# Exponentials of the windowed attention on one engine or two, two more borrowed load buffers, and an even cut of the widest score row

## The chip, the cores and the metric

The kernel runs on 1 core of one Trainium2 chip. The metric is device time in microseconds (us), the median over runs of the whole kernel. The engines are PE (matrix multiplications and transposes), DVE (vector), ACT (scalar functions), POOL and SP (which only issues DMA here).

## The reference, cut to what matters

Three layers follow one another, over 4 batches of 576 positions with model width 512.

- **Windowed attention**, 8 heads of width 64. Heads 0 to 3 see the 32 positions up to their own; heads 4 to 7 see every fourth of the 128 positions up to their own. `attn = exp(scores - max) / (sum + 1e-9)`, then `attn @ v`.
- **A mixture of 4 causal attention experts** (head width 64, all 576 positions): `q = x @ wq[e]`, `scores = q @ k.T / 8`, causal mask, softmax, `@ v @ wo[e]`. A gate takes the best 2 of 4 experts for each position and weights them by a softmax.
- **A normalized MLP** with residual: `x + relu(norm(x) @ w_ch1) @ w_ch2`, hidden width 2048.

Everything is computed in float32. A large product is made as three products of a high and a low part (hence names such as `xh` and `xl`, `wkh` and `wkl`).

## The kernel before, in words

**One list orders everything.** The program is written as many small generators, called chains, one for each piece of work: `turned_qk`, `scores`, `window` for the windowed layer, `project`, `attend`, `out_proj` for the experts, `decode`, `norm_tile`, `mlp_group` for the MLP. Each step of a chain names an engine, a planned duration and the times of what it depends on. `run_chains` keeps a planned clock for each engine (`free`) and always emits the step that can start first; the rank of the chain breaks ties. The planned durations therefore decide in which order each engine gets its instructions, and on the chip each engine works through its own order and waits where a dependence is late. A step made with `either(...)` may go to one of two engines; the list compares their start times and takes the first named where they are equal. PSUM is handed out as 8 banks by `acq("bank")` and `give_bank`.

**Windowed layer.** Work goes by head pair `hp` (0 to 3) of batch `b`. `load_qk` loads q and k of a pair (288 KB each) from SP into two tiles tagged `nat`; there are two such tiles in all, so the next pair waits until the transposes of `turned_qk` (line 442) have read this one. For batch 0, pairs 1 and 2 use pieces 0 to 7 of `x2a` instead, which holds the mixture's output later. `load_v` loads v into one of two `vt` places and waits for a place that the multiplications by v (line 565) of an earlier pair have left. `all_loads` is one chain: its loads stand in SP's queue in a fixed order, pair by pair, q and k before v. `landing` plans when a load has arrived: 600 ns, then 4.76 ns for each KB behind the loads before it, then 1200 ns. `turned_qk` transposes q and k and copies them (`ptr` to `qT`, `kT`) by ACT or DVE; `scores` (lines 490 to 504) forms the masked scores of a pair in two banks; `window` handles one of the two halves `u`, so there are 4 x 4 x 2 = 32 such blocks. A block has 6 groups of 80 columns (dilated pairs) or 5 or 4 groups of 96 columns. In each: DVE takes the maximum of each group (line 525) and subtracts it (527), ACT takes the exponential of the whole block (530), DVE sums and inverts (532, 534), DVE or POOL multiplies (536), PE transposes (548), ACT or DVE copies (251), PE multiplies by v (565), ACT and DVE split the result into `xh` and `xl` (579, 581).

**Experts.** `project` makes queries and keys (line 706), `value_tile` values and gate logits (605), and `attend` handles one block of 128 queries for two experts. The last block (i = 4) has 576 columns and does not fit one bank of 512, so its scores (lines 778, 779, mask 781) are cut in two: columns 0 to 64 and 64 to 576, with a maximum (801) and an exponential (806) for each. There are 2 x 2 x 4 = 16 such rows of scores. `out_proj` (929) writes pieces of `x2a`.

**MLP.** Lines 1157 and 1179; it begins while the last batch's experts still run.

Of the kernel before, what the change touches and what calls it, by code (L numbers as in the profile page):

```python
# [23 lines left out]
def windowed_attention_moe_mlp(  # L24
# [37 lines left out]
    QB = 8  # L62
    SCALE = 0.125
    DQ, DW = 48, 80
    NBD = S // DQ

    def qrange(i):
# [97 lines left out]
    def op(engine, ns, deps=(), tile=None):  # L165
        return "op", ((engine, ns),), deps, tile
# [4 lines left out]
    def acq(tag, n=1):  # L171
        return "acq", tag, n
# [4 lines left out]
    def give(tag, at, n=1):  # L177
        places[tag] += [at] * n

    def give_bank(b, at):  # L180
        places["bank"].append((at, lent_banks.pop(id(b))[0]))
# [7 lines left out]
    def act(n, psum=True):  # L189
        return (55.0 if psum else 100.0) + 0.835 * n  # L190

    def dve(n):
        return 65.0 + 1.045 * n

    def turn(n):
        return 0.834 * n + 2.5
# [7 lines left out]
    def run_chains():  # L204
        while chains:
            again = True
            while again:
                again = False
                for c in sorted(chains, key=lambda c: c[0]):
                    kind = c[2][0]  # L210
                    if kind == "acq" and len(places[c[2][1]]) >= c[2][2]:
                        tag, n = c[2][1:]
                        places[tag].sort()
                        at = places[tag][n - 1]
                        if tag == "bank":
                            taken.extend(x for _, x in places[tag][:n])
                            at = at[0]
                        del places[tag][:n]
                        resume(c, at)
                        again = True  # L220
                        break
                    if kind == "key" and c[2][1] in facts:
                        resume(c, facts[c[2][1]])
                        again = True
                        break
            best = None
            for c in chains:
                if c[2][0] != "op":
                    continue
                _, engines, deps, tile = c[2]  # L230
                for name, ns in engines:
                    engine = name.rstrip("*")
                    at = max([free[engine]] + [d + lag[engine] for d in deps])
                    if name != engine:
                        at = max(at, shared["POOL" if engine == "DVE" else "DVE"])
                    change = MODE if engine == "PE" and tile != mode[0] else 0.0
                    score = (at + change + (ns if len(engines) > 1 else 0.0) * 0.0, c[0])
                    if best is None or score < best[0]:
                        best = score, c, name, ns, at + change, tile
            assert best is not None, [(c[0], c[2]) for c in chains]  # L240
            _, c, name, ns, at, tile = best
            engine = name.rstrip("*")
            if name != engine:
                shared[engine] = at + ns + 80.0
            free[engine] = at + ns
            if engine == "PE":
                mode[0] = tile
            resume(c, (at + ns + tail[engine], engine) if len(c[2][1]) > 1 else at + ns + tail[engine])
# [72 lines left out]

    SLOT = (3, 2, 4, 1, 5, 0, 6, 7, 8)

    def landing(t, kb):

        land[0] = max(t + 600.0, land[0]) + 4.76 * kb
        return land[0] + 1200.0

    def issue(e, dst, src):
# [8 lines left out]
    def load_qk(b, hp, engines="SS"):  # L338
        h0 = 2 * hp
        cw = 8 if h0 >= H // 2 else 6  # L340
        pw = S // cw
        lent = b == 0 and hp in (1, 2)
        t = (yield acq("nat", 2)) if not lent else 0.0
        nats, times = [], []
        for x, src in enumerate((q, k)):
            if lent:
                nat = x2a[:, 4 * hp - 4 + 2 * x:4 * hp - 2 + 2 * x].rearrange("p a n -> p (a n)")
            else:
                nat = win.tile([P, 2 * DM], F32, tag="nat", name="nat", bufs=2)
            nat = nat[:pw, :cw * 2 * D].rearrange("p (c h d) -> p c h d", c=cw, h=2)  # L350
            e = "ACT" if engines[x] == "A" else "SP"
            ti = yield op(e, 780.0, [t])
            issue(e, nat, src[b, h0:h0 + 2].rearrange("h (p c) d -> p c h d", c=cw))
            nats.append(nat)
            times.append(landing(ti, 288.0))
        LD[b, hp] = nats, times
        put("ld", b, hp, at=0.0)
# [65 lines left out]
    def turned_qk(b, hp):  # L423

        yield key("ld", b, hp)
        nats, times = LD[b, hp]
        tq = yield acq("qT")
        qT = win.tile([P, S], F32, tag="qT", name=f"qT{b}_{hp}", bufs=2)
        kT = win.tile([P, W + S], F32, tag="kT", name=f"kT{b}_{hp}", bufs=2)
        yield op("POOL", 130.0, [tq])  # L430
        nc.gpsimd.memset(kT[:, 0:W], 0.0)
        dil = 2 * hp >= H // 2
        cw = 8 if dil else 6
        pw, ch = S // cw, cw // 2
        ends = []
        for x in range(4):
            nat, hf = nats[x // 2], x % 2
            ta = yield acq("bank")
            pt = bank("ptr")
            t = yield op("PE", ch * turn(pw), [ta, times[x // 2]])  # L440
            for c in range(ch):
                nc.tensor.transpose(pt[:, pw * c:pw * (c + 1)],  # L442
                                    nat[:, hf * ch + c].rearrange("p h d -> p (h d)"), ident[:pw, :pw])
            if hf and not (b == 0 and hp in (1, 2)):
                give("nat", t)
            dst = kT[:, W:] if x > 1 else qT
            if dil:
                dst = dst.rearrange("p (c j x) -> p x c j", c=4, x=2)[:, hf]
                sp = pt[:, :HS].rearrange("p (c j) -> p c j", c=4)
            else:  # L450
                dst = dst.rearrange("p (j c) -> p j c", c=cw)[:, :, hf * ch:(hf + 1) * ch]
                sp = pt[:, :HS].rearrange("p (c j) -> p j c", c=ch)
            if x > 1:
                t, e = yield either(("ACT", 345.0), ("DVE", 366.0), deps=[t, tq])
                copy_by(e, dst, sp)
            else:
                t, e = yield either(("ACT", 345.0), ("DVE", 366.0), deps=[t, tq])
                if e == "ACT":
                    nc.scalar.mul(dst, sp, SCALE)
                else:  # L460
                    nc.vector.tensor_scalar(dst, sp, SCALE, None, op0=ALU.mult)
            give_bank(pt, t)
            ends.append(t)
        TQ[b, hp] = qT, kT
        put("qT", b, hp, at=max(ends))
# [44 lines left out]
    def window(b, hp, u):  # L510
# [11 lines left out]
        sc = sx[:, :nb, off:96]  # L522
        mx, sm, rs = [win.tile([P, NBD // NU], F32, tag=x, name=x, bufs=5)[:, :nb] for x in ("mx", "sm", "rs")]
        t = yield op("DVE", dve(kw * nb), [t])
        nc.vector.tensor_reduce(mx, psv, axis=AX.X, op=ALU.max)
        t = yield op("DVE", dve(kw * nb), [t, ts])
        nc.vector.tensor_tensor(sc, psv, mx[:, :, None].to_broadcast([P, nb, kw]), op=ALU.subtract)
        give_bank(ps, t)
        t = yield op("ACT", act(kw * nb, False), [t])
        nc.scalar.activation(sc, sc, AF.Exp)  # L530
        t = yield op("DVE", dve((kw + 1) * nb), [t])
        nc.vector.tensor_reduce(sm, sx[:, :nb, off:], axis=AX.X, op=ALU.add)
        t = yield op("DVE", 85.0, [t])
# [24 lines left out]
        vt, tv, home = LV[b, hp]  # L558
        ta = yield acq("bank")
        po = bank("po")  # L560
        t = yield op("PE", nb * (91.0 if dil else 114.0), ends + [ta, tv], "columns")
        for tt, t_ in enumerate(blk):
            for h in range(2):
                z = side(u, HALVES[h]).start // 64
# [187 lines left out]
    def attend(b, pr_, i):  # L752
# [16 lines left out]
        Pp = att.tile([P, 2, S], F32, tag="P", name="Pp", bufs=DB + 1)  # L769
        Ps, tsum = [], []  # L770
        for ee in range(2):
            cuts = [(0, n)] if n <= 512 else [(0, 64), (64, n)]
            tb = yield acq("bank", len(cuts))
            pss, tss = [bank("s2") for _ in cuts], []
            for (a, z), ps in zip(cuts, pss):
                end = z == n
                t = yield op("PE", 2 * max(0.4415 * (z - a) + 5.0, 90.0) + (55.0 if end else 0.0), [tb, tq])
                nc.tensor.matmul(ps[:m, :z - a], SQ[ee][:, q0:q0 + m], KH[ee][:, a:z], start=True, stop=False)  # L778
                nc.tensor.matmul(ps[:m, :z - a], SQ[ee][:, q0:q0 + m], KL[ee][:, a:z], start=False, stop=not end)  # L779
                if end:  # L780
                    nc.tensor.matmul(ps[:m, q0 - a:z - a], ident_bf, mdiag[:, :n - q0], start=False, stop=True)  # L781
                tss.append(t)
# [123 lines left out]
    def out_proj(b, i):  # L906
# [10 lines left out]
        if ti >= NTA:  # L917

            yield key("fr", b, (ti - NTA) // 2)
        elif HOME[ti] >= LENT:  # L920
            for hp in range(NHP):
                t = max(t, (yield key("x", B - 1, hp)))
# [345 lines left out]
```

## Time and profile before

| what | value |
|---|---|
| median of 3 runs | 723.19 us (722.45 to 726.18) |
| the profiled execution's own time | 725.05 us |
| its span, first to last instruction | 723.3 us |
| mean granted clock of TensorE | 0.995 |
| PE busy in the span | 700.0 us (97%) |
| DVE, ACT, POOL busy | 524.5, 287.0, 165.1 us |

Time outside the span is 725.05 - 723.3 = 1.75 us. Busy time of PE is the time in which some matmul was under way, from its start to its modelled end; matmuls overlap, so the rate is read from one start to the next, not from the duration. In rows of a timeline an idle time before an instruction stands in brackets with what ended it. "SPq" is SP issuing a DMA.

### The profile page before, as it was taken

The numbers are of one execution on the slowest core, as the hardware profiler recorded it, in microseconds if no ns is written. First come the engines' busy times: TensorE is split into PE (matmuls) and PEld (weight loads), VectorE is DVE, ScalarE is ACT, GpSimd is POOL, SyncE is SP. The second block draws the span as 40 slices with busy tenths as digits, with TensorE's granted clock in tenths as the row PEclk, the third lists the DMA queues.
The fourth block names the chain that finished last, engine by engine and source line by source line (L and its number), as shares of the span: only waits on it lengthen the run. The fifth ranks groups of instructions, "written<-read, shape, count | busy, mean of one in ns | idle before, by whom it ended". The sixth has DMA issues, their size and how long they took to land.

```text
span 723.3 us, 13830 instructions
## 1 busy us (share of the span) xinstructions
PE 700.0 (97%) x5396; PEld 588.5 (81%) x5396; DVE 524.5 (73%) x1240; ACT 287.0 (40%) x754; POOL 165.1 (23%) x190
## 2 busy tenths in 40 slices
PE   6799999999999999999999999999999999999997
PEld 4788787988898888877878888888888888888886
DVE  4759879968989999994588874774774865844343
ACT  3566757656656667851242231220221211311100
POOL 3641113110011325220035351230330420410000
PEclk9999999999999999999999999999999999999999
DMA  9953541033312112000002121020110110100123
GB/s 166 200 134 83 115 102 46 18 67 74 82 42 69 38 47 68 30 30 1 1 29 88 59 87 30 30 86 2 59 58 1 61 56 12 47 1 1 58 88 116
DMA packets 78385, 43.10 MB, mean 60 GB/s; under 512 B 60145, under 2 KB 73713, under 8 KB 78321
## 3 DMA queue, kind: packets, MB, share of 16 engines
q1 hardware_dynamic: 78320, 42.23, 23.2%
q8 instruction: 42, 0.69, 0.4%
q14 instruction: 23, 0.18, 0.1%
HBM read 35.14 MB, written 4.72 MB: 55 GB/s over the span
## 4 chain that ended last, share of the span: by engine, by line
PE 84%; DVE 5%; DMA 4%; ACT 3%; SPq 2%; issue 1%; POOL 0%; ACTq 0%; DVEq 0%; POOLq 0%
PE phid L1157 28%; PE pout L1179 28%; PE pp L706 5%; PE pv L605 3%; PE pwo L929 3%; PE ppt L854 2%; DMA nat<-in_q_dram 2%; PE po L565 2%; PE ppt L548 2%; PE py L875 2%; SPq L330 2%; PE s L778 2%; PE s L779 2%; PE ptr L442 2%; PE py L873 1%; PE s L504 1%
## 5 line engine op out<-in xcount | busy, mean ns | idle before, releaser
L1179 PE MATMUL pout<-wp,ht 128*128 128x512 f32 x864 | 220.1, 395 | 0.0
L1157 PE MATMUL phid<-xn,wp 128*128 128x512 f32 (+1 forms) x960 | 218.9, 371 | 0.0
L1157 PEld LDWEIGHTS phid<-xn,wp 128*128 128x128 f32 x960 | 168.8, 188 | 34.4
L1179 PEld LDWEIGHTS pout<-wp,ht 128*128 128x128 f32 x864 | 160.0, 188 | 35.1 <-ACT ht L1162 0.2
L1162 ACT ACTIVATE ht<-phid 128x512 fp32r<-128x512 f32 (+1 forms) x80 | 44.4, 554 | 225.1 <-PE phid L1157 225.1
L1188 DVE SCALAR_TENSOR_TENSOR x2a<-pout,rstd,x2a 128x512 f32<-128x512 f32 x124 | 92.5, 748 | 53.9 <-PE pout L1179 53.1
L1164 DVE SCALAR_TENSOR_TENSOR ht<-phid,ht 128x512 fp32r<-128x512 f32 (+1 forms) x80 | 50.8, 635 | 58.6 <-ACT ht L1162 57.9
L1031 POOL TENSOR_TENSOR d_pw<-d_pw,d_t 128x512 f32<-128x512 f32 x32 | 41.6, 1299 | 184.9 <-DVE d_pw L1028 151.7
L1043 POOL TENSOR_TENSOR wp<-d_pw,wp 128x512 fp32r<-128x512 f32 x32 | 44.3, 1384 | 45.7 <-ACT wp L1041 45.7
L536 POOL TENSOR_TENSOR sc<-sc,rs 128x480 f32<-128x480 f32 (+1 forms) x24 | 22.9, 963 | 88.2 <-DVE rs L534 62.8
L251 ACT COPY pT<-ppt 80x288 f32<-80x288 f32 (+6 forms) x77 | 32.1, 426 | 19.5 <-PE ppt L854 9.9
L1015 ACT ACTIVATE d_sq<-ws 128x512 f32<-128x512 f32 x32 | 21.6, 676 | 44.0 <-DVE d_pw L1034 25.3
L794 ACT ACTIVATE Pp<-s,nm 128x448 f32<-128x448 f32 (+3 forms) x64 | 30.3, 476 | 12.5 <-DVE nm L792 11.5
L1041 ACT CAST wp<-d_pw 128x512 fp32r<-128x512 f32 x32 | 19.9, 621 | 35.6 <-DVE d_pw L1034 32.9
L778 PE MATMUL s<-KH,SQ 128*128 128x64 f32 (+4 forms) x96 | 32.6, 347 | 0.2
L1034 DVE SCALAR_TENSOR_TENSOR d_pw<-d_sq,d_pw 128x512 f32<-128x512 f32 x32 | 22.0, 689 | 14.7 <-POOL d_pw L1031 14.7
L442 PE MATMUL ptr<-ident,nat 72*128 72x72 f32 (+1 forms) x196 | 24.4, 246 | 7.2 <-DMA nat<-in_q_dram 6.4
L548 PE MATMUL ppt<-ident,sc 112*80 112x112 f32 (+1 forms) x168 | 27.2, 282 | 3.9 <-POOL sc L536 2.4
L779 PE MATMUL s<-klz,SQ 128*128 128x64 f32 (+4 forms) x96 | 30.2, 315 | 0.0
L1188 DVE SCALAR_TENSOR_TENSOR x2b<-pout,rstd,x2b 128x512 f32<-128x512 f32 x32 | 24.0, 749 | 8.4 <-PE pout L1179 8.2
L854 PE MATMUL ppt<-ident,Pp 128*128 128x128 f32 x160 | 28.5, 283 | 0.4 <-DVE yl L892 0.2
L792 DVE TENSOR_REDUCE nm<-s 128x1 f32<-128x448 f32 (+3 forms) x64 | 26.3, 415 | 3.1 <-PE s L781 2.3
(166 smaller groups left out, 1294.9 us busy)
## 6 DMA issues: line engine op xcount, KB each, us to landing
ws<-in_moe_w_ch_dram SPq DMA_DIRECT2D x32, 512.0 KB, 3.5
nat<-in_q_dram SPq DMA_DIRECT2D x14, 288.0 KB, 4.0
nat<-in_k_dram SPq DMA_DIRECT2D x14, 288.0 KB, 6.6
out_dram<-x2a SPq DMA_DIRECT2D x12, 256.0 KB, 2.0
KH<-KH SPq DMA_DIRECT2D x32, 72.0 KB, 1.9
vt<-in_v_dram SPq DMA_DIRECT2D x10, 192.0 KB, 3.9
x2a<-in_v_dram SPq DMA_DIRECT2D x8, 160.0 KB
vt<-in_v_dram SPq DMA_DIRECT2D x8, 160.0 KB
```

Source lines behind the costliest of these rows:

```text
L442: nc.tensor.transpose(pt[:, pw * c:pw * (c + 1)], nat[:, hf * ch + c].rearrange("p h d -> p (h d)"), ident[:pw, :pw])
L548: nc.tensor.transpose(pt[:kw, P * (tt - a):P * (tt - a) + pw], sc[:pw, tt], ident[:pw, :pw])
L778: nc.tensor.matmul(ps[:m, :z - a], SQ[ee][:, q0:q0 + m], KH[ee][:, a:z], start=True, stop=False)
L779: nc.tensor.matmul(ps[:m, :z - a], SQ[ee][:, q0:q0 + m], KL[ee][:, a:z], start=False, stop=not end)
L854: nc.tensor.transpose(pt[:, P * (j - 1):P * j], Ps[ee][:, k0:k0 + P], ident)
L1031: nc.gpsimd.tensor_tensor(pf, pf, t1.bitcast(F32), op=ALU.add)
L1043: nc.gpsimd.tensor_tensor(lo, pf, hi.bitcast(F32), op=ALU.subtract)
L1157: nc.tensor.matmul(ph[:, :n_tok], ws[:, c * P:(c + 1) * P], xs[c], start=n == 0, stop=n == 3 * KC - 1)
L1162: nc.scalar.activation(hh[:, :n_tok], ph[:, :n_tok], AF.Relu)
L1164: nc.vector.scalar_tensor_tensor(hl[:, :n_tok], ph[:, :n_tok], 0.0, hh[:, :n_tok].bitcast(F32), op0=ALU.max, op1=ALU.subtract)
L1179: nc.tensor.matmul(po, a_[:, sl], w_, start=n == 0, stop=n == 3 * len(fs) - 1)
L1188: nc.vector.scalar_tensor_tensor(x2(i), po, rstd[:, i:i + 1], x2(i), op0=ALU.mult, op1=ALU.add)
```

## The change

- `window`: the maximum is stored negated. The subtraction on DVE becomes an addition, or the list gives the block to ACT alone, which then takes one exponential for each group, straight out of PSUM, with the negated maximum as bias. The list picks the engine that can start first; `LEAN` is 0, so DVE is taken where both can start at the same time. In the first way the bank is handed back after DVE's addition, in the second after the last exponential.
- `load_qk`: batch 1's pairs 1 and 2 also use pieces 0 to 7 of `x2a`, and wait for the transposes of batch 0's same pair. `out_proj` into these pieces waits until batch 1's pair has been transposed.
- `attend`: the last block's scores are cut into columns 0 to 288 and 288 to 576.
- Planned durations: 5.4 instead of 4.76 ns per KB of a load, and the issuing queue's planned clock is held to 3200 ns before the planned end of its transfers; 25 ns more for the transposes of q and k; 110 instead of 91 ns for each dilated group of the multiplication by v; 100 instead of 55 ns for the score rows' mask.

```diff
     DQ, DW = 48, 80
+    LEAN = 0.0
...
-                for name, ns in engines:
+                for name, ns, *lean in engines:
...
-                    score = (at + change + (ns if len(engines) > 1 else 0.0) * 0.0, c[0])
+                    score = (at + change + sum(lean), c[0])
...
-    def landing(t, kb):
-
-        land[0] = max(t + 600.0, land[0]) + 4.76 * kb
+    def landing(t, kb, e="SP"):
+
+        land[0] = max(t + 600.0, land[0]) + 5.4 * kb
+        free[e] = max(free[e], land[0] - 3200.0)
         return land[0] + 1200.0
...
-        lent = b == 0 and hp in (1, 2)
-        t = (yield acq("nat", 2)) if not lent else 0.0
+        lent = b < 2 and hp in (1, 2)
+        if not lent:
+            t = yield acq("nat", 2)
+        else:
+            t = (yield key("nq", 0, hp)) if b else 0.0
...
-            t = yield op("PE", ch * turn(pw), [ta, times[x // 2]])
+            t = yield op("PE", ch * turn(pw) + 25.0, [ta, times[x // 2]])
...
-            if hf and not (b == 0 and hp in (1, 2)):
+            if hf and not (b < 2 and hp in (1, 2)):
                 give("nat", t)
+            if x == 3:
+                put("nq", b, hp, at=t)
...
-        nc.vector.tensor_reduce(mx, psv, axis=AX.X, op=ALU.max)
-        t = yield op("DVE", dve(kw * nb), [t, ts])
-        nc.vector.tensor_tensor(sc, psv, mx[:, :, None].to_broadcast([P, nb, kw]), op=ALU.subtract)
-        give_bank(ps, t)
-        t = yield op("ACT", act(kw * nb, False), [t])
-        nc.scalar.activation(sc, sc, AF.Exp)
+        nc.vector.tensor_reduce(mx, psv, axis=AX.X, op=ALU.max, negate=True)
+        t, e = yield either(("DVE", dve(kw * nb), 0.0), ("ACT", nb * 222.0, LEAN), deps=[t, ts])
+        if e == "DVE":
+            nc.vector.tensor_tensor(sc, psv, mx[:, :, None].to_broadcast([P, nb, kw]), op=ALU.add)
+            give_bank(ps, t)
+            t = yield op("ACT", act(kw * nb, False), [t])
+            nc.scalar.activation(sc, sc, AF.Exp)
+        else:
+            for tt in range(nb):
+                nc.scalar.activation(sc[:, tt], psv[:, tt], AF.Exp, bias=mx[:, tt:tt + 1])
+            give_bank(ps, t)
...
-        t = yield op("PE", nb * (91.0 if dil else 114.0), ends + [ta, tv], "columns")
+        t = yield op("PE", nb * (110.0 if dil else 114.0), ends + [ta, tv], "columns")
...
-            cuts = [(0, n)] if n <= 512 else [(0, 64), (64, n)]
+            cuts = [(0, n)] if n <= 512 else [(0, HS), (HS, n)]
...
-                t = yield op("PE", 2 * max(0.4415 * (z - a) + 5.0, 90.0) + (55.0 if end else 0.0), [tb, tq])
+                t = yield op("PE", 2 * max(0.4415 * (z - a) + 5.0, 90.0) + (100.0 if end else 0.0), [tb, tq])
...
+        elif ti < 8:
+            t = max(t, (yield key("nq", 1, 1 + ti // 4)))
```

## Rows read from the trace of the kernel before

**Rows 1.** Busy time in stretches: columns PE, PEld, DVE, ACT, POOL, clock, DMA, GB/s.
```profile
82.00:86.00 4.00, 2.52 (x47) 2.08 (x42) 3.36 (x11) 2.20 (x8) 0.99 (x1) 0.77 1.07 217
40.00:250.00 210.00, 203.12 (x2571) 180.30 (x2568) 181.57 (x575) 134.62 (x405) 36.04 (x60) 0.99 0.32 74
370.00:723.30 353.30, 349.40 (x1604) 287.40 (x1602) 220.00 (x333) 68.68 (x122) 83.34 (x65) 1.00 0.15 50
```
**Rows 2.** The page's first part: busy time of PE over the span.
```profile
PE 700.0 (97%) x5396; PEld 588.5 (81%) x5396; DVE 524.5 (73%) x1240; ACT 287.0 (40%) x754; POOL 165.1 (23%) x190
```
**Rows 3.** Waits of PE over the whole span: total us, times, longest.
```profile
PE ptr L442 <- DMA nat<-in_q_dram: 6.4, 3, 5.0
PE ppt L548 <- POOL sc L536: 2.4, 5, 0.8
PE s L504 <- ACT kT L251: 1.5, 1, 1.5
```
**Rows 4.** Timeline of PE, last block's scores in batch 3: start, duration.
```profile
238.84 0.19 PE L778 MATMUL s<-KH,SQ 128*128 128x64 f32 x1
...
238.98 0.47 PE L778 MATMUL s<-KH,SQ 128*128 128x512 f32 x1
239.29 0.39 PE L779 MATMUL s<-klz,SQ 128*128 128x512 f32 x1
239.52 0.23 PE L781 MATMUL s<-mdiag,ident_bf 128*128 128x128 bf16 x1
```
**Rows 5.** Chain of waits, a run of projections with 288 columns: start, length.
```profile
141.21 1.58 PE pp L706 x12
```
**Rows 6.** Groups of instructions by shape on DVE and ACT: busy us, mean ns.
```profile
L527 DVE TENSOR_TENSOR sc<-s,mx 128x480 f32<-128x480 f32 x24 | 15.3, 646 | 0.1
L530 ACT ACTIVATE sc<-sc 128x480 f32<-128x480 f32 x24 | 14.2, 606 | 5.0 <-DVE sc L527 4.8
L794 ACT ACTIVATE Pp<-s,nm 128x192 f32<-128x192 f32 x16 | 6.7, 420 | 4.3 <-DVE nm L792 3.8 <-DVE rs L818 0.4
L794 ACT ACTIVATE Pp<-s,nm 128x64 f32<-128x64 f32 x16 | 5.0, 315 | 1.4 <-DVE nm L792 1.0
```
**Rows 7.** Timelines of DVE and ACT, two such blocks back to back.
```profile
29.35 1.21 DVE L527 TENSOR_TENSOR sc<-s,mx 128x480 f32<-128x480 f32 x2
31.31 1.10 ACT L530 ACTIVATE sc<-sc 128x480 f32<-128x480 f32 x2
```
**Rows 8.** Timeline of ACT and PE around PE's wait for kT.
```profile
81.20 1.10 ACT L530 ACTIVATE sc<-sc 128x480 f32<-128x480 f32 x2
...
82.80 0.78 ACT L251 COPY kT<-ptr 128x288 f32<-128x288 f32 x2
...
83.73 1.13 PE L504 MATMUL s<-kT,qT 64*64 64x96 f32 x29 [1.48 <-ACT kT L251]
```
**Rows 9.** Timeline of SP: loads of batch 1 in the order of the queue.
```profile
31.17 3.72 SPq L330 DMA_DIRECT2D x2a<-in_v_dram  x3
39.55 0.59 SPq L330 DMA_DIRECT2D nat<-in_q_dram  x1
...
47.75 0.84 SPq L330 DMA_DIRECT2D nat<-in_q_dram  x1
...
60.21 1.28 SPq L330 DMA_DIRECT2D x2a<-in_v_dram  x3
61.54 0.86 SPq L330 DMA_DIRECT2D nat<-in_q_dram  x1
```
**Rows 10.** Timeline of PE: batch 1's first scores, then transposes of its pairs 1 and 3.
```profile
44.55 0.23 PE L495 MATMUL s<-mfirst,ident_bf 64*64 64x96 bf16 x2 [0.78 <-DVE xl L581]
...
45.24 0.35 PE L496 MATMUL s<-mgen,ident_bf 64*64 64x384 bf16 x2 [0.30 <-DVE xl L581]
...
46.22 0.30 PE L442 MATMUL ptr<-ident,nat 96*128 96x96 f32 x1
...
67.34 0.44 PE L442 MATMUL ptr<-ident,nat 72*128 72x72 f32 x4 [1.07 <-DMA nat<-in_q_dram]
```

## The prediction

> **What bounds the kernel now.** First the busy time of the engines over the span: PE has a matmul under way for 700.0 of 723.3 us [rows 2], so at most 23.3 us are open gaps. Next the stretches [rows 1]. From 370 us to the end the MLP runs alone, with PE busy for 349.4 of 353.3 us; no edit touches an instruction there. The 32 windowed blocks lie before about 250 us. From 40 to 250 us PE is busy for 203.1 of 210 us, DVE for 181.6 (86%) and ACT for 134.6 (64%). So DVE is the fuller of the two helpers, yet PE sets the pace: work taken off DVE earns only where PE waited for it. An edit can pay in three ways: fewer columns or less dead time on PE itself, a wait of PE that goes, or a stretch at the lower clock that goes.
>
> Then the waits of PE [rows 3]. The largest, 6.4 us for q, holds 5.0 us for the very first load, which nothing here changes; 1.4 us are left. 2.4 us are waits for POOL's multiply, which stands behind DVE's sums. 1.5 us is one wait for a copy of k on ACT, and the timeline shows why [rows 8]: two whole-block exponentials hold ACT from 81.20 us, the copies start at 82.80, PE starts at 83.73. In 82 to 86 us the granted clock is 0.77 [rows 1]. The levels are 1.2 and 2.4 GHz, that is 0.5 and 1.0, so this mean hides a spell at 1.2 GHz, after a gap of PE; it costs up to 4.0 x 0.23 = 0.9 us.
>
> **The even cut of the widest score row.** It happens 16 times. Now four matmuls (two of 64, two of 512 columns) take from 238.84 to the mask at 239.52, that is 0.68 us [rows 4]. The new four have 288 columns each, 1152 in all as before. Twelve of 288 columns take 1.58 us in a dense run [rows 5], so four take 0.53 and save 0.15 us. But the second matmul of the wide pair starts 0.31 us after the first, and the next after it 0.23 us later: there are some 0.08 us of dead time where the shape changes, and part of this may stay. I take 0.10 x 16 = 1.6 us; bounds 0 and 0.15 x 16 = 2.4 us. DVE and ACT see the same columns in the same number of instructions, so I cost that at nothing.
>
> **Exponentials on ACT alone.** Per block that changes side, DVE loses an addition of 0.646 us [rows 6]; two of them take 1.21 us back to back [rows 7], so they overlap by 0.08 and DVE's queue gains 0.56. On ACT, exponentials with a bias from PSUM take 315 ns at 64 columns and 420 at 192 [rows 6], or 0.82 ns per column: 341 ns at 96, 328 at 80. Two in a row overlap by 2 x 0.606 - 1.10 = 0.11 us [rows 6, 7]. Five groups of 96 take 5 x 0.341 - 4 x 0.11 = 1.27 us, six of 80 take 1.42 us, against 0.606 now. ACT is longer by 0.66 to 0.81 us per block. From the maximum to the finished exponential the two ways are about equal: 0.646 + 0.606 = 1.25 us against 1.27 to 1.42.
>
> The Trainium skill (ScalarE: Activation LUTs, section "What ACT_TABLE_LOAD costs") speaks against this split: every exponential with a pointer as bias has a fixed 280 ns beside 0.833 ns per column, and neighbours overlap by 93 ns. By that a block would be an estimated 1.43 us (5 x 96) or 1.62 us (6 x 80), some 0.2 us dearer on ACT; in the sum only ACT's load would differ, by about 3 us over 16 blocks. The row at 64 columns, 315 ns, is below the page's 333, and the sum stays with the rows.
>
> How many of the 32 go to ACT, the trace can't show: between 0 and 32. The list takes the engine that can start first, and right behind the maximum DVE's planned queue is the fuller one; where both are free it is DVE. I take half, 16: DVE loses 9.0 us of its 181.6, ACT gains some 12 on 134.6 (70% of the stretch). Both still fit under PE. What it earns is a share of PE's waits behind DVE: 2.4 for the multiply, 1.5 for the copy of k and the 0.9 us of clock behind it, 4.8 us in all. POOL's own multiply (unchanged) and the residuals of the weights still stand in part of the first, and the second is a queue on ACT which can also become longer. I take 1.8 us; bounds +4.8 us and, if ACT becomes the late one, a loss of 4 us (below: six waits of 0.7). The bank is held for 1.3 instead of 0.65 us; what would queue behind it is the next pair's scores, which wait for banks already once [rows 10]. The negated maximum costs nothing: it is the same instruction.
>
> **Two more borrowed buffers and the planned loads.** Batch 1's pair 1 is issued from 39.55 us on, though the loads ahead of it in SP's queue were out at 31.17 + 3.72 = 34.9 us [rows 9]: it waits for the two staging tiles. Borrowed pieces free it some 5 us earlier; its other condition, the transposes of batch 0's pair, is long met. Its transposes begin at 46.22 us, right behind two gaps of 0.78 and 0.30 us [rows 10] that they could have filled. Pair 2 (47.75) gains little, for v stands ahead of it. Pair 3 (61.54) gains nothing: it follows v at 60.21, which waits for a place of v, and PE waits 1.07 us for it at 67.34 [rows 9, 10]. The longer planned transfer puts 576 KB 0.64 x 576 = 370 ns later in the plan, so PE is given other work for about 0.4 us of that wait. Together I take 0.8 + 0.4 = 1.2 us; bounds 2.5 us (both gaps and the whole remaining 1.4) and a loss of 1 us, if the later plan moves work ahead of transposes that were ready. `out_proj` waits for batch 1's transposes, done by some 60 us; its first piece comes more than a batch later, so this costs nothing unless batch 1 is moved behind it. The other planned durations emit no instruction; they move the order, and the new order can't be read here; I allow 1 us either way for it, the size of one gap of [rows 10].
>
> **Sum.** 1.6 + 1.8 + 1.2 = 4.6 us off the profiled execution's 725.05 us, or 720.45. That execution lies 1.9 us above the median of the runs, 723.19, so on the scale of the median the forecast is 718.6 us.
>
> **The rivals.**
>
> *Only PE's own work counts.* DVE's relief lies off the path, as the 97% of PE say, the gaps move elsewhere when the order changes, or the list never gives a block to ACT, because at equal starts DVE goes first. Then the cut alone is left: 723.2 - 1.6 = 721.6 us. For it: only 4.8 us of waits and clock name this chain at all. Against it: in 40 to 250 us DVE is at 86% and its queue is in the order of everything else. Chance 0.33.
>
> *ACT becomes the late engine.* Place: the copies of q, k and of the transposed exponentials, which PE waits for and which queue behind an ACT block, as in [rows 8]. There ACT held PE for 1.48 us behind 1.10 us of exponentials; a block on ACT is 1.3 to 1.4 us without a break and 0.7 us longer than now. If 9 of 16 blocks put their 0.7 us on PE, and one more gap brings the low clock for 0.9 us, that is 7.2 us, less 1.6 for the cut and 1.2 for the loads: +4.4, 727.6 us. It decides from about four blocks on, where the loss passes the 2.8 us of the other two edits. For it: ACT's longest wait on PE's path today is just this one. Against it: ACT has 36% of the stretch free, and the list plans 222 ns a group, close to 341 - 110 = 231. Chance 0.15.
>
> *DVE really paces the windowed stage.* Then half of DVE's 9.0 us come back, 4.5 in place of 1.8, and the borrowed buffers let the next pair run ahead (2.5): 1.6 + 4.5 + 2.5 = 8.6, 714.6 us. For it: the 86% is a mean, with copies that ACT may now give way to. Against it: PE gaps of that size are not in the list of waits outside the first loads. Chance 0.10.
>
> **How the numbers follow.** The forecast has the other 0.42, its own range is 716.5 to 720.5 us. A change of 0.5% is 3.6 us, about what a measurement of this kernel can tell from none: faster is below 719.6, slower above 726.8. Of the forecast's 0.42 some 0.33 lie below 719.6; with the 0.10 that is 0.43 for faster. The rest of it and the first rival give 0.42 for the same, the second 0.15 for slower. The range that leaves out the slow rival and the far end of the fast one is 714.5 to 725.0 us; beyond the rivals it also holds the sum with any one term at its end.
>
> **What the profile after would show.** Exponentials of 128x80 and 128x96 on ACT at 0.33 to 0.34 us each, for some 16 blocks, and as many fewer additions on DVE. Score rows of 288 columns with 0.55 to 0.6 us from first matmul to mask. Batch 1's pair 1 loaded at about 35 us, into `x2a`, and transposed before 45. PE's wait for POOL's multiply below 2.4 us in total. In 370 us to the end of before, the same length of MLP. The prediction is wrong if PE waits for ACT's copies by more than 1.5 us in total, if fewer than five or more than 25 blocks go to ACT, or if a second spell at 1.2 GHz appears after 40 us.

## The result, and the profile after

The changed kernel takes 716.15 us (median of 6 runs, 713.73 to 716.90) against 723.52 us (6 runs, 722.45 to 726.18): 7.4 us less, ratio 0.9888 with a 95% interval of 0.9864 to 0.9911. The profiled execution took 713.73 us with a span of 712.0 us, where the one before took 725.05 and 723.3.

First the page's line of busy times after the change, then the span with the mean granted clock, and the stretches (columns as in [rows 1]).

```profile
PE 693.6 (97%) x5396; PEld 585.8 (82%) x5396; DVE 512.3 (72%) x1214; ACT 299.4 (42%) x838; POOL 169.8 (24%) x198
```
```profile
core 0: 712.0 us, clock 0.999
```
```profile
20.00:40.00 20.00, 18.02 (x326) 16.03 (x314) 11.72 (x26) 13.47 (x41) 12.97 (x20) 1.00 0.98 198
80.00:100.00 20.00, 19.80 (x273) 18.07 (x272) 15.20 (x53) 13.14 (x46) 3.75 (x8) 1.00 0.44 94
40.00:250.00 210.00, 207.35 (x2603) 186.70 (x2600) 181.51 (x590) 151.47 (x495) 43.91 (x64) 1.00 0.31 72
82.00:86.00 4.00, 3.80 (x65) 3.40 (x62) 3.91 (x14) 3.23 (x9) 1.39 (x4) 1.00 0.40 91
```

Open time without any matmul in 40 to 250 us fell from 6.9 us [rows 1] to 2.65 us. ACT carries 151.5 us there instead of 134.6, and DVE no less than before, because more work now fits into the same stretch. The spell at the lower clock in 82 to 86 us is gone. The kernel before had two such spells; two wider stretches of its trace hold one each:

```profile
20.00:40.00 20.00, 15.77 (x231) 13.96 (x225) 13.03 (x30) 11.83 (x31) 13.09 (x19) 0.91 0.90 171
80.00:100.00 20.00, 18.46 (x228) 16.40 (x224) 15.45 (x48) 13.20 (x41) 3.28 (x6) 0.91 0.47 102
```

A mean of 0.91 over 20 us costs up to 0.09 x 20 = 1.8 us at full speed, so the two cost up to 3.6 us; the changed kernel has 1.00 in both.

The waits of PE after the change, its four largest and further down those for other copies on ACT (line 252), and one row of the same view of the kernel before:

```profile
PE ptr L447 <- DMA nat<-in_q_dram: 4.8, 1, 4.8
PE ppt L560 <- POOL sc L548: 2.1, 2, 1.3
PE pxt L1121 <- ACT xg L1114: 1.2, 3, 0.5
PE po L577 <- ACT pT L252: 0.9, 1, 0.9
PE pp L718 <- ACT pT L252: 0.7, 1, 0.7
...
PE ptr L447 <- ACT kT L252: 0.4, 1, 0.4
...
PE s L511 <- ACT kT L252: 0.2, 1, 0.2
```
```profile
PE ppt L548 <- ACT pT L251: 1.0, 1, 1.0
```

Against [rows 3]: the later waits for q are gone, POOL's multiply is nearly as it was, and the scores' wait of 1.5 us for the copy of k on ACT is down to 0.2 us. All rows of this view add up to 13.8 us, where the 20 of before gave 19.1.

The gain is complete before the MLP runs alone. The last `out_proj` matmul, before and after:

```profile
362.57 0.39 PE L929 MATMUL pwo<-woh,yl 128*128 128x512 f32 x1
```
```profile
351.23 0.39 PE L943 MATMUL pwo<-woh,yl 128*128 128x512 f32 x1
```

It comes 11.3 us earlier, and 723.3 - 362.6 = 360.7 us follow before, 712.0 - 351.2 = 360.8 us after. In both traces 207 matmuls of the MLP stand ahead of it, so the same work follows.

The widest score row, in the last batch after the change and, of the kernel before, one that was not shown:

```profile
244.84 0.38 PE L790 MATMUL s<-KH,SQ 128*128 128x288 f32 x1
245.06 0.29 PE L791 MATMUL s<-klz,SQ 128*128 128x288 f32 x1
245.19 0.29 PE L790 MATMUL s<-KH,SQ 128*128 128x288 f32 x1
245.32 0.29 PE L791 MATMUL s<-klz,SQ 128*128 128x288 f32 x1
245.46 0.23 PE L793 MATMUL s<-mdiag,ident_bf 128*128 128x128 bf16 x1
```
```profile
106.16 0.28 PE L778 MATMUL s<-KH,SQ 128*128 128x64 f32 x1
106.27 0.28 PE L779 MATMUL s<-klz,SQ 128*128 128x64 f32 x1
106.39 0.47 PE L778 MATMUL s<-KH,SQ 128*128 128x512 f32 x1
106.70 0.39 PE L779 MATMUL s<-klz,SQ 128*128 128x512 f32 x1
106.93 0.23 PE L781 MATMUL s<-mdiag,ident_bf 128*128 128x128 bf16 x1
```

From the first start to the mask: 0.62 us after, 0.77 us in this row before. [Rows 4] (0.68 us) was one of the shortest. Over the rows whose five matmuls follow one another in the trace, the mean is 0.76 us before (14 rows, 0.68 to 0.87) and 0.59 us after (15 rows, 0.53 to 0.63): 0.17 x 16 = 2.8 us.

The exponentials of the windowed blocks on ACT, by shape, and two blocks from the timeline:

```profile
L541 ACT ACTIVATE sc<-s,mx 128x96 f32<-128x96 f32 x60 | 15.3, 360 | 5.8 <-DVE mx L532 5.8
L541 ACT ACTIVATE sc<-s,mx 128x80 f32<-128x80 f32 x48 | 11.4, 346 | 5.4 <-DVE mx L532 5.1 <-DVE rs L546 0.3
L538 ACT ACTIVATE sc<-sc 128x480 f32<-128x480 f32 x8 | 5.0, 625 | 0.7 <-DVE sc L535 0.6
L538 ACT ACTIVATE sc<-sc 128x384 f32<-128x384 f32 x3 | 1.6, 532 | 0.2
```
```profile
14.64 1.27 ACT L541 ACTIVATE sc<-s,mx 128x96 f32<-128x96 f32 x5 [1.26 <-DVE mx L532]
...
26.82 1.42 ACT L541 ACTIVATE sc<-s,mx 128x80 f32<-128x80 f32 x6 [1.51 <-DVE mx L532]
```

11 blocks kept the old way (the two rows of L538), so 21 of 32 went to ACT alone.

Loads of batch 1 after the change, from SP's timeline, and the first transposes of pair 1 from PE's:

```profile
33.97 0.59 SPq L332 DMA_DIRECT2D x2a<-in_q_dram  x1
...
42.61 0.84 SPq L332 DMA_DIRECT2D x2a<-in_q_dram  x1
...
60.02 0.86 SPq L332 DMA_DIRECT2D nat<-in_q_dram  x1
```
```profile
40.35 0.41 PE L447 MATMUL ptr<-ident,x2a 96*128 96x96 f32 x3
```

Pair 1 is issued 5.6 us and transposed 5.9 us earlier than in [rows 9, 10]. Pair 2, which the prediction expected to gain little, is issued 5.1 us earlier (42.61 against 47.75).

A rough account of the 11.3 us between the two spans: up to 3.6 us of lower clock, 2.8 us of shorter score rows, 19.1 - 13.8 = 5.3 us of waits; 11.7 in all. It says what went between these two executions, not which edit removed it. The profiled execution before lies 1.5 us above its median and the one after 2.4 us below its own, so 3.9 of the 11.3 us belong to the choice of executions and not to the 7.4 us of the change. Which edit gave what is for the experiments.

### The profile page after: what moved, and what is told of

It reads as the page before. It is cut to its first block, busy times and chain, and to the rows that moved or that the text cites. A ratio compares the mean times of both kernels' runs of the same rounds, so it can differ in the third digit from the quotient of the medians.

```text
span 712.0 us, 13890 instructions
## 1 busy us (share of the span) xinstructions
PE 693.6 (97%) x5396; PEld 585.8 (82%) x5396; DVE 512.3 (72%) x1214; ACT 299.4 (42%) x838; POOL 169.8 (24%) x198
## 4 chain that ended last, share of the span: by engine, by line
PE 82%; DVE 9%; ACT 3%; issue 2%; SPq 1%; DMA 1%; POOL 1%; DVEq 0%; POOLq 0%; ACTq 0%
PE pout L1193 28%; PE phid L1171 28%; PE pp L718 5%; PE pv L617 3%; PE pwo L943 3%; PE ppt L866 2%; PE ptr L447 2%; PE po L577 2%; PE py L887 2%; PE ppt L560 2%; PE s L790 1%; PE s L511 1%; PE s L791 1%; PE py L885 1%; ACT Pp L806 1%
## 5 line engine op out<-in xcount | busy, mean ns | idle before, releaser
L1057 POOL TENSOR_TENSOR wp<-d_pw,wp 128x512 fp32r<-128x512 f32 x32 | 42.8, 1338 | 43.2 <-ACT wp L1055 43.2
L548 POOL TENSOR_TENSOR sc<-sc,rs 128x480 f32<-128x480 f32 (+1 forms) x28 | 26.8, 966 | 63.7 <-DVE rs L546 20.7
L252 ACT COPY pT<-ppt 80x288 f32<-80x288 f32 (+7 forms) x76 | 33.1, 447 | 14.5 <-PE ppt L866 10.1
L806 ACT ACTIVATE Pp<-s,nm 128x64 f32<-128x64 f32 (+3 forms) x64 | 30.6, 479 | 13.0 <-DVE nm L804 10.9
L541 ACT ACTIVATE sc<-s,mx 128x96 f32<-128x96 f32 (+1 forms) x108 | 26.6, 354 | 11.3 <-DVE mx L532 10.9
L790 PE MATMUL s<-KH,SQ 128*128 128x288 f32 (+4 forms) x96 | 31.2, 330 | 0.1
L1035 DVE SCALAR_TENSOR_TENSOR d_t<-ws,d_t 128x512 int32<-128x512 int32 x32 | 28.7, 896 | 0.4
L791 PE MATMUL s<-klz,SQ 128*128 128x288 f32 (+4 forms) x96 | 28.5, 302 | 0.0
L804 DVE TENSOR_REDUCE nm<-s 128x1 f32<-128x64 f32 (+3 forms) x64 | 25.7, 415 | 3.4 <-PE s L793 2.9
```

The costliest lines, as they stand in the source:

```text
L806: nc.scalar.activation(Pt[:m, :n], pss[0][:m, :n], AF.Exp, bias=nm[:m, ee:ee + 1], accum_out=sm[:m, ee:ee + 1])
L1057: nc.gpsimd.tensor_tensor(lo, pf, hi.bitcast(F32), op=ALU.subtract)
```

## The experiments

Every kernel was timed in 5 rounds beside the kernel before on the same chip. The first four put one part of the change alone into the kernel before, the next four take one part out of the changed kernel. The changed kernel was not timed again beside them; the kernel before read 723.5 us beside it, 723.8 beside experiments 5 to 8 and 724.4 beside 9 to 12, so a distance from the changed kernel is uncertain by about as much. `plan` below means all the planned durations.

**1. The exponentials alone.**

```diff
-        nc.vector.tensor_tensor(sc, psv, mx[...], op=ALU.subtract)
+        t, e = yield either(("DVE", dve(kw * nb), 0.0), ("ACT", nb * 222.0, LEAN), deps=[t, ts])
...
+                nc.scalar.activation(sc[:, tt], psv[:, tt], AF.Exp, bias=mx[:, tt:tt + 1])
```

> Kernel before with one part alone: the list may give a block's exponentials to ACT. Theory of waits (DVE's relief removes PE's waits on the windowed chain, the spell at 1.2 GHz behind 82 us with them): 2 to 4 us below before, some 16 to 22 of 32 blocks on ACT, no spell at 1.2 GHz between 40 and 370 us. Rival, the order (each edit only reshuffles the list, what is gained is the luck of the new order): within 1 us of before. Rival, ACT late: 2 us or more above before, with PE waiting for copies on ACT by more than 3 us.

Measured: 721.01 us against 723.73, ratio 0.9962 (0.9946 to 0.9978): 2.7 us less. 72 exponentials of 80 columns and 51 of 96 ran on ACT, 23 blocks. That is what the theory of waits expected, one block aside. Its stretches:

```profile
20.00:40.00 20.00, 16.68 (x225) 14.82 (x224) 12.45 (x28) 13.39 (x45) 10.87 (x17) 0.83 0.99 184
40.00:370.00 330.00, 323.46 (x3366) 276.52 (x3365) 272.42 (x824) 215.32 (x677) 61.54 (x79) 1.00 0.25 57
```

The spell behind 82 us is gone, as expected, but the one in the opening is longer: it costs up to 0.17 x 20 = 3.4 us instead of 1.8.

**2. The even cut alone.**

```diff
-            cuts = [(0, n)] if n <= 512 else [(0, 64), (64, n)]
+            cuts = [(0, n)] if n <= 512 else [(0, HS), (HS, n)]
```

> Kernel before with one part alone: the widest score rows cut at 288. Theory of waits: 1.6 us below before (0 to 2.4), 0.55 to 0.6 us from the first matmul of the row to its mask instead of 0.68. Rival, the order: anywhere within 2 us of before, on either side, with the same 0.1 us per row.

Measured: 718.34 us, ratio 0.9922 (0.99 to 0.9944): 5.4 us less. That is outside both expectations. The rows themselves became shorter by 0.17 us as in the whole change, 2.8 us. The other 2.6 us are not in the rows. The list works out a row's planned duration from its widths, 697 ns for the old cut and 584 for the new (from the code), so this edit moves the order too; which wait the 2.6 us come from was not traced. They are not the clock. Two stretches of its trace, and the wait for the copy of k that [rows 8] show for the kernel before:

```profile
20.00:40.00 20.00, 16.99 (x214) 14.88 (x213) 12.11 (x28) 11.08 (x29) 12.38 (x18) 0.74 0.88 172
80.00:100.00 20.00, 18.47 (x244) 16.54 (x240) 15.35 (x48) 13.81 (x43) 3.28 (x6) 1.00 0.47 102
```
```profile
83.69 1.04 PE L505 MATMUL s<-kT,qT 64*64 64x96 f32 x36 [1.48 <-ACT kT L252]
```

The opening loses up to 0.26 x 20 = 5.2 us here, more than both spells of the kernel before (3.6), and the kernel is still 5.4 us faster. And the wait of 1.48 us for k is still there, without a spell at the lower clock behind it.

**3. The borrowed buffers alone.**

```diff
-        lent = b == 0 and hp in (1, 2)
+        lent = b < 2 and hp in (1, 2)
...
```

> Kernel before with one part alone: two pairs of batch 1 in borrowed pieces. Theory of waits: 0.8 us below before (up to 2), pair 1 issued at about 35 us and transposed before 45 us. Rival, the order: within 2 us of before, on either side. Rival that the loads are hidden anyway: within 0.5 us of before.

Measured: 723.60 us, ratio 0.9986 (0.9968 to 1.0005): no difference that can be told. Pair 1 is issued at 33.89 us and transposed from 44.95 us, as expected, and the two gaps of [rows 10] are not among its waits any more. All waits of PE add up to 17.8 us against 19.1, but the clock in its stretches of 20 us from 20 to 60 and from 80 to 100 us is 0.89, 0.94 and 0.91: up to 5.2 us lost against 3.6.

**4. The planned durations alone.**

```diff
-        land[0] = max(t + 600.0, land[0]) + 4.76 * kb
+        land[0] = max(t + 600.0, land[0]) + 5.4 * kb
+        free[e] = max(free[e], land[0] - 3200.0)
...
-            t = yield op("PE", ch * turn(pw), [ta, times[x // 2]])
+            t = yield op("PE", ch * turn(pw) + 25.0, [ta, times[x // 2]])
```

(with 110 for 91 and 100 for 55 ns)

> Kernel before with one part alone: the planned durations (5.4 ns per KB and the held queue, 25 ns on transposes, 110 and 100 ns); the instructions are the same as before, in another order. Theory of waits: 0.4 us below before, at most 1. Rival, the order: 3 us or more below before, most of what the whole change gave.

Measured: 717.70 us, ratio 0.9909 (0.9883 to 0.9935): 6.0 us less, with no edit to the work itself. The rival, the order, predicted this and the theory of waits did not.

**5. Everything but the exponentials.**

```diff
-        t, e = yield either(("DVE", dve(kw * nb), 0.0), ("ACT", nb * 222.0, LEAN), deps=[t, ts])
...
+        t = yield op("DVE", dve(kw * nb), [t, ts])
+        nc.vector.tensor_tensor(sc, psv, mx[...], op=ALU.subtract)
...
```

> Changed kernel without ACT's exponentials (every block adds on DVE). Theory of waits: 719 to 720.5 us, that is 3 to 4 us above the changed kernel's 716.15. Rival, the order: within 1 us of the changed kernel.

Measured: 720.86 us, 4.7 us above the changed kernel and just above the 719 to 720.5 of the theory. Its trace has the later spell at the lower clock again, behind a wait of 1.83 us for POOL's multiply:

```profile
80.00:100.00 20.00, 17.39 (x209) 15.54 (x208) 16.92 (x58) 14.75 (x46) 5.39 (x8) 0.91 0.44 91
```
```profile
83.78 0.48 PE L555 MATMUL ppt<-ident,sc 112*80 112x112 f32 x3 [1.83 <-POOL sc L543]
```

with PE busy for 17.4 of 20 us, where the changed kernel has 19.8 and 1.00. The spell costs up to 1.8 of the 4.7 us.

**6. Everything but the cut.**

```diff
-            cuts = [(0, n)] if n <= 512 else [(0, HS), (HS, n)]
+            cuts = [(0, n)] if n <= 512 else [(0, 64), (64, n)]
```

> Changed kernel with the widest score rows cut at 64 as before. Theory of waits: 1.6 us above the changed kernel, 717.8 us (716 to 718.5). Rival, the order: anywhere within 2 us of it.

Measured: 717.53 us, 1.4 us above the changed kernel, near the 1.6 of the theory but also within the 2 us of the rival. The ratios to the kernel before, 0.9910 (0.9891 to 0.9930) and 0.9888 (0.9864 to 0.9911), overlap, so the 1.4 us are not clear of noise. In this order the rows take 0.73 us on the mean (14 rows, 0.68 to 0.78), so they are longer by 0.14 x 16 = 2.2 us, not by 2.8.

**7. Everything but the borrowed buffers.**

```diff
-        lent = b < 2 and hp in (1, 2)
+        lent = b == 0 and hp in (1, 2)
...
```

> Changed kernel without batch 1's borrowed pieces. Theory of waits: 0.8 to 2 us above the changed kernel. Rival that these loads are hidden anyway: within 0.5 us of it.

Measured: 715.24 us, 0.9 us below the changed kernel, with ratios to the kernel before of 0.9883 (0.9861 to 0.9906) and 0.9888 (0.9864 to 0.9911) that can't be told apart. With experiment 3: the buffers gave nothing that can be told.

**8. Everything but the planned durations.**

```diff
-        land[0] = max(t + 600.0, land[0]) + 5.4 * kb
-        free[e] = max(free[e], land[0] - 3200.0)
+        land[0] = max(t + 600.0, land[0]) + 4.76 * kb
```

(and the other three as before)

> Changed kernel with the planned durations of before. Theory of waits: 0.4 us above the changed kernel, at most 1. Rival, the order: 3 us or more above it.

Measured: 718.80 us, ratio 0.9936 (0.9914 to 0.9957), 2.7 us above the changed kernel, between the two theories. In its trace 20 to 40 us has a mean clock of 0.83, up to 3.4 us.

The four single gains add up to 2.7 + 5.4 + 0.1 + 6.0 = 14.2 us, the whole change gave 7.4. What each costs when it is left out adds up to 4.7 + 1.4 - 0.9 + 2.7 = 7.9. The three edits that gain alone thus give less together, as they would if they removed partly the same loss (which loss, these runs don't show), and a new theory was needed: either the planned loads repair the opening, or any new order helps.

**9. The planned loads alone.** The first three lines of experiment 4's diff.

```diff
-        land[0] = max(t + 600.0, land[0]) + 4.76 * kb
+        land[0] = max(t + 600.0, land[0]) + 5.4 * kb
+        free[e] = max(free[e], land[0] - 3200.0)
```

> Kernel before with the planned loads alone (5.4 ns per KB, the issuing queue's planned clock held); same instructions, another order. Theory of the planned loads: the gain of the planned durations is made in the opening, because steps that need late loads no longer stand ahead of steps that are ready; then 718 to 720 us, and the first projection starts 3 us or more before the 48.1 us of the kernel before. Rival, the luck of the order: any new order gives something between -6 and +1 us, in any stage; then the first projection may start when it likes.

Measured: 732.19 us against 724.36, ratio 1.0124 (1.01 to 1.0148): 7.8 us more. Both theories of the expectation fell. The first projection did start early, at 43.70 us instead of 48.13, as the theory of the planned loads asked, and the time was lost all the same. The stretches of its trace from 20 to 100 us, its waits for POOL's multiply (5 of them, 2.9 us the longest), and the matmul at which one of them ended:

```profile
20.00:40.00 20.00, 17.91 (x238) 16.27 (x230) 11.48 (x25) 11.57 (x30) 14.08 (x22) 0.83 0.87 176
40.00:60.00 20.00, 16.68 (x249) 15.03 (x248) 14.40 (x39) 10.96 (x29) 7.55 (x13) 0.90 0.57 123
60.00:80.00 20.00, 20.00 (x263) 19.02 (x261) 11.85 (x34) 11.13 (x32) 1.61 (x4) 0.84 0.35 89
80.00:100.00 20.00, 17.13 (x191) 15.07 (x191) 15.77 (x51) 14.36 (x43) 4.62 (x9) 0.83 0.32 68
```
```profile
PE ppt L550 <- POOL sc L538: 8.3, 5, 2.9
```
```profile
55.23 1.88 PE L550 MATMUL ppt<-ident,sc 128*96 128x128 f32 x9 [2.51 <-POOL sc L538]
```

The clock is low in all four stretches: up to 0.17 x 20 + 0.10 x 20 + 0.16 x 20 + 0.17 x 20 = 12.0 us lost, against 3.6 in the kernel before. The 8.4 us between are about the 7.8 that the time grew by. In 60 to 80 us PE is busy throughout and still at 0.84: the spell began right behind the 2.51 us for which PE stood until 55.23.

**10. The other planned durations alone.**

```diff
-        t = yield op("PE", nb * (91.0 if dil else 114.0), ends + [ta, tv], "columns")
+        t = yield op("PE", nb * (110.0 if dil else 114.0), ends + [ta, tv], "columns")
```

(with 25 ns more for transposes and 100 for 55 ns)

> Kernel before with the other planned durations alone (25 ns on transposes, 110 for 91 ns, 100 for 55 ns). Theory of the planned loads: the opening stays as before (first projection within 1 us of 48.1 us), and the time within 1.5 us of before. Rival, the luck of the order: 718 us or so, like the planned durations as a whole and like the cut alone.

Measured: 721.77 us, ratio 0.9967 (0.9945 to 0.999): 2.6 us less. First projection at 45.8 us, 2.3 earlier than before, so the opening did not stay. Between both expectations; together with 9 it shows that -2.6 and +7.8 make -6.0.

**11. A nudge.**

```diff
-            t = yield op("PE", ch * turn(pw), [ta, times[x // 2]])
+            t = yield op("PE", ch * turn(pw) + 3.0, [ta, times[x // 2]])
```

> Kernel before with 3 ns more planned for the transposes of q and k and nothing else: a nudge that says nothing about the chip and only breaks ties another way. If the order before was an unlucky one (rival, the luck of the order): 2 us or more below before. Theory that the parts work by what they say: within 1 us of before.

Measured: 724.33 us against 724.36, ratio 1.0004 (0.9984 to 1.0023). This one other order is no better, so the order before was not simply an unlucky one that any other beats; one nudge shows no more than that.

**12. All 32 blocks on ACT.**

```diff
-        t, e = yield either(("DVE", dve(kw * nb), 0.0), ("ACT", nb * 222.0, LEAN), deps=[t, ts])
+        t, e = (yield op("ACT", nb * 222.0, [t, ts])), "ACT"
```

> Changed kernel with all 32 blocks' exponentials on ACT instead of 21. Theory of waits: DVE gets another 11 x 0.56 = 6 us, ACT some 8 us more, PE's waits for ACT grow: 1 to 3 us above the changed kernel. Rival that DVE paces the windowed stage: 1 us or more below it. Rival, ACT becomes the late engine: 4 us or more above it.

Measured: 721.11 us, 5.0 us above the changed kernel. Its stretch from 20 to 40 us, the matmul behind the longest wait, and ACT, DVE and POOL ahead of it:

```profile
20.00:40.00 20.00, 17.75 (x239) 15.75 (x236) 11.47 (x26) 12.97 (x45) 12.59 (x19) 0.74 1.01 200
```
```profile
26.30 0.77 PE L560 MATMUL ppt<-ident,sc 112*80 112x112 f32 x6 [2.02 <-POOL sc L548]
```
```profile
20.84 1.40 ACT L541 ACTIVATE sc<-s,mx 128x80 f32<-128x80 f32 x6
...
22.40 1.48 ACT L541 ACTIVATE sc<-s,mx 128x80 f32<-128x80 f32 x6
...
25.78 2.73 ACT L541 ACTIVATE sc<-s,mx 128x80 f32<-128x80 f32 x12 [1.02 <-DVE mx L532]
```
```profile
23.43 1.23 DVE L544 TENSOR_REDUCE sm<-sc 128x6 f32<-128x486 f32 x2
...
24.90 0.25 DVE L546 RECIPROCAL rs<-sm 128x6 f32<-128x6 f32 x2
```
```profile
25.25 1.94 POOL L548 TENSOR_TENSOR sc<-sc,rs 128x480 f32<-128x480 f32 x2
```

PE stood for 2.02 us, from 24.28 us on, and the stretch has a mean clock of 0.74: up to 0.26 x 20 = 5.2 us, as much as the whole difference. But the wait was not for exponentials. Those of the two blocks were done at 22.24 and 23.88 us, before it began. DVE, busy without a break there, summed them from 23.43 us on and inverted at 24.90, and POOL multiplied from 25.25. ACT itself then stood idle for 1.02 us, for DVE's next maximum.

## Why the prediction was right in time and wrong in part

The forecast was 718.6 us with 714.5 to 725.0; measured 716.15. Point by point:

- **What bounds the kernel.** Right. What follows the last `out_proj` matmul kept its 360.7 us, and the gain came before it: rows, waits and lower clock of PE.
- **The even cut, 1.6 us.** The mechanism was right, the term too small: 2.8 us in the rows, above its upper bound of 2.4. The step that failed is the choice of one row to price all 16: [rows 4] begins with a 64-column matmul that is followed after 0.03 us, while 0.11 us is usual, as in the row at 106.16 us. What the cut gives to the whole depends on the order around it, 5.4 us alone and some 1.4 us inside.
- **Exponentials on ACT, 1.8 us.** The price per block was exact: 1.27 us for five groups and 1.42 us for six, as worked out. 21 blocks instead of 16 changed side. The worth was too small: 2.7 us alone and 4.7 us inside the change, near the upper bound. The wait of 1.5 us for the copy of k is gone, and so is the spell at the lower clock behind it; that the one brought the other is not shown, for experiment 2 has the wait without the spell. The prediction had multiply, copy and spell as one term of 4.8 us and took 1.8. The Trainium skill (ScalarE: Activation LUTs, section "What ACT_TABLE_LOAD costs") gave 280 + 0.833 ns per column, that is 360 and 347 ns, and the rows show 360 and 346, closer than the 341 and 328 read off the accumulated exponentials. But its overlap of 93 ns is too small here: (5 x 360 - 1270) / 4 = 132 ns. The two deviations cancel in the prediction's block times.
- **ACT as the late engine.** It did not happen with 21 blocks, though it was put at about four. With all 32 the time rose by 5.0 us (experiment 12), as far as the rival asks, but not by its mechanism: the wait ahead of the slow stretch hung on DVE and POOL, not on a copy on ACT. That another 11 blocks off DVE gained nothing speaks against the rival that DVE paces the stage, though in that one wait DVE was the late engine. Between 21 and 32 blocks nothing was tried.
- **Borrowed buffers, 0.8 us.** Wrong. Pair 1 came as early as forecast, and taking the buffers away cost nothing (experiments 3 and 7). The failed step is that the gaps of [rows 10] were counted as time to be won: in experiment 3 they went, and other waits and a lower clock took their place.
- **Planned loads and durations, 0.4 us.** This is the step that failed by most: "they move the order, and the new order can't be read here; I allow 1 us either way for it". The whole of them gives 6.0 us alone and 2.7 us inside. Yet their two halves alone change the time by -2.6 and +7.8 us. Being truer about loads is not what earns: that half is the one that loses. They choose another order, and orders differ by up to 14.5 us (717.7 to 732.2) with the same work but for the free choices of engine.
- **The clock.** Priced at 0.9 us for one spell, from a stretch of [rows 1] that ends inside it; the kernel before has two, up to 3.6 us, and the changed kernel has none in these stretches. In experiments 9 and 12 lost clock is as large as the loss, in 5 it is less than half of it. It is not what the edits earn: experiments 2 and 4 gain 5.4 and 6.0 us at a median clock of 0.994, which the kernel before has beside them too. Nor does an order fix its spells. The 29 executions of the kernel before that stand beside experiments 9 to 12 have mean clocks from 0.989 to 1.000; the ten at 0.997 or above have a median of 722.3 us, the 14 from 0.993 to 0.996 one of 724.5. The changed kernel, at 0.997 to 0.999, has 716.15. So the clock explains some 1 to 2 of the 7.4 us.
- **The prediction's own signs.** It called itself wrong if PE waited for ACT's copies by more than 1.5 us in total. These waits add up to 0.9 + 0.7 + 0.4 + 0.2 = 2.2 us, so the sign came; it was badly set, since the kernel before has 1.5 + 1.0 = 2.5 us of them. The other two signs, on the blocks and on a second spell, did not come.

So the total is near partly by luck. Cut, exponentials and order were put too low and buffers too high, and the prediction added terms that don't add: 14.2 us singly, 7.4 together. Small terms and a sum without overlap offset each other. What stays open is why one order has long waits and another none. That the halves of the planned durations add up to +5.2 us and both together give -6.0 was only measured, not traced step by step.

## What to carry to other kernels

Where one list with planned durations orders all engines, price an edit of these durations as a new order: here between -6 and +8 us, as much as any edit of the work gave alone. Allow for the clock that a wait of PE may cost behind it, but compare several executions before calling it the cause. Read a cost from several rows of a group before multiplying it; and measure parts both alone and left out, because parts need not add (here 14.2 us singly, 7.4 together).

## What the runs showed of the hardware that was not expected

- A wait of PE can be followed by a long spell at the lower level although PE is then busy: in experiment 9, behind a wait of 2.51 us, means of 0.90 in 40 to 60 us and 0.84 in 60 to 80 us, the latter with 20.00 of 20 us busy, make (0.10 + 0.16) x 20 x 2 = 10 us at 1.2 GHz. It need not be: the wait of 1.48 us for k has a spell behind it in the kernel before and none in experiment 2, and in experiment 8 PE waits for 2.23 us until 80.12 us, with a clock of 1.00 in 60 to 100 us. Experiment 10 has 0.91 in 80 to 100 us, and its longest wait apart from those for q is 0.8 us. What brings a spell is not shown here.
- Neighbouring exponentials from PSUM with a bias overlap by 132 ns (5 of 96 columns, 360 ns each, in 1.27 us), those of whole blocks before by 110 ns [rows 6, 7].
- A 64-column pair beside a 512-column pair costs 0.77 us with its mask in the usual case, four equal matmuls of 288 columns 0.53 to 0.63 us, for the same number of columns.
